# An S4 layer beside a SiLU feed-forward: decays made ahead of the filter's generation, tables in one pass, spectral operands split a step earlier

## The chip, the core and the metric

The kernel runs on one core of one Trainium2 chip. The metric is the device time of one execution in microseconds; of several executions the median counts. A core has five engines that run side by side, each with an instruction queue of its own that is worked in order: TensorE (PE in the profile, its weight loads PEld), VectorE (DVE), ScalarE (ACT), GpSimd (POOL) and SyncE (SP), which here only issues DMAs. They wait for one another through semaphores.

## The reference

```python
xn = _layernorm(x, axis=-1)                       # x: 1 x 2048 x 576
return x + _A_ref(xn, ...) + _B_ref(xn, w1, w2)

# _A_ref: a state-space layer as a long convolution, D = 576 channels, N = 128 states
dt = exp(log_dt)[:, None]; A = A_re + 1j*A_im; Bc, Cc likewise
P = exp((dt*A)[:, :, None] * l)                   # l = 0 .. 2047
K = einsum("dn,dnl,dn->dl", Cc, P, dt*Bc).real    # one filter of 2048 taps per channel
y = irfft(rfft(u, 4096) * rfft(K, 4096))[:2048] + u * Dskip

# _B_ref: feed-forward, F = 4608
out = silu(x @ w1) @ w2
```

All data is float32.

## The kernel before

There are two strands of work. The **feed-forward strand** (`ffn`, L223) is TensorE's main load: nine chunks of 512 hidden columns for each of four row blocks of 512 (two halves of two), 36 blocks of eight steps. `up` makes 512 columns of `ph` with 14 matmuls (L281 to L283), ScalarE applies SiLU (`gf`, L289) and rounds the result to a short float32 form (`gh`, L290), VectorE forms the rest (`gl`, L291). `down` multiplies with w2 (`po`, L306), and VectorE adds each `po` to the accumulator (L310). Every operand is split in a high and a low part (`w1h`/`w1l`, `w2h`/`w2l`), so that each product takes three matmuls. In one block the order is u0, d0, d1, d2, d3, u1, u2, u3, where the u steps belong to the next block.

The **side strand** (`side`, L699) holds all else, in stages:

- `phase0` normalises two row tiles at a time and turns them for the matmuls (`pt`, L118 and L122); tiles 8 to 15 go to DRAM (`dxt`) for the second half.
- `natural` (L370) makes tables from the parameters with states on the free axis: the real rate `lr`, the frequency `f`, the magnitude `rho` and the phase `phi` of C times B. It runs twice, each time over three of the six channel groups (96 x 384 elements an instruction), with a square root and an arctangent on ScalarE, which need other activation tables than SiLU, and turns the tables on TensorE (`ptk`, L452).
- `kgen` (L455) generates the filter in 36 chunks of 16 channels. For a pair of chunks `powers` makes the four decays of each state from `lr`: a product (L484), tanh(x/2) on ScalarE (L485), then (1 + t) / (1 - t) with a reciprocal (L486, L487, L490), then powers up to the seventh (L492 to L494). `head` and the lines after it make sine and cosine tables (L501 to L521), and VectorE multiplies them with the decays into S and C (L522 to L538). TensorE contracts them (`kp`, L558), and turns the result by a small DFT (`z`, L573); the outcome goes to DRAM (`d1k`). Beside it, `spread` does the same first DFT step for the input (`pu`, L149 and L150, to `d1u`).
- `spectral` (L592) has 32 steps. `front(k)` loads and splits the operands from `d1u` and `d1k`, multiplies each with a DFT matrix (`pk`, `pu`), and forms their complex product `y`; the next matmuls (`pb`) turn it back, and it is written to `d2`. `front(k + 1)` stands ahead of the second half of step k.
- `tail` (L637) loads `d2` as `ys` (`conv_load`), and `add_conv` applies the last DFT step (`py`, L691) for the first eight row tiles. For the last eight, `add_conv` is part of the last block's `down`.

What sets the order: `weave` (L31) advances the side strand when the feed-forward strand has made a given share of its 288 steps; the shares of the stages are the tuple `marks` (L701). A planner that runs the program against its own costs then writes the order of each engine's queue; `tc.high_priority()` and `behind(...)` (not before a given instruction) bend it. A pool's tile with `bufs=n` has n buffers, and a writer waits for the readers of the buffer that it takes over.

Of the kernel before, what the change touches and what calls it, by code (L numbers as in the profile page):

```python
# [17 lines left out]
P = 128  # L18
L = 2048
D = 576  # L20
# [21 lines left out]
def kernel(  # L42
# [40 lines left out]
    dr0 = dram.tile([8 * P, D], F32, name="dr0")  # L83

# [6 lines left out]
    nc.vector.memset(halfpi, math.pi / 2)  # L91
    mhalf = cst.tile([P, 2], F32, name="mhalf")
# [76 lines left out]
    def norm(p0, js, xs):  # L169
# [12 lines left out]
        xn = p0.tile([P, 2, D], F32, tag="xn", name="xn")  # L182
# [40 lines left out]
    def ffn():  # L223
# [38 lines left out]
        def split_w2(half, c, t):  # L262
            first = half == 0 and c == 0
            r2 = R2.pop((half, c, t))
            h2 = wp.tile([P, D], F32R, tag="w2h", name="w2h", bufs=FT + 1)
            l2 = wp.tile([P, D], F32R, tag="w2l", name="w2l", bufs=FT + 1)
            with behind(pins["xt_s"] if first else pins["gh"]):
                nc.scalar.copy(h2, r2)  # L268
# [101 lines left out]
    def natural(nat):  # L370
        lrT, fT, rhoT, phiT = (kf[n] for n in ("lr", "f", "rho", "phi"))
        for half in range(2):
            NT = 3
            NP = 96
            ts = slice(half * NT, (half + 1) * NT)

            def load(ap, name):
                t = nat.tile([NP, NT, NS], F32, tag=name, name=name)
                nc.sync.dma_start(t, ap.rearrange("(p t) n -> p t n", t=6)[:, ts, :])
                return t  # L380

            are, aim = load(a_re, "are"), load(a_im, "aim")
            br, bi = load(b_re, "br"), load(b_im, "bi")
            cr, ci = load(c_re, "cr"), load(c_im, "ci")
            dt = nat.tile([NP, NT], F32, tag="dt", name="dt")
            nc.sync.dma_start(dt, log_dt.rearrange("(p t) -> p t", t=6)[:, ts])

            e1 = nat.tile([NP, NT], F32, tag="e1", name="e1")
            e2 = nat.tile([NP, NT], F32, tag="e2", name="e2")
            ec = float(np.float32(math.e))  # L390
            nc.vector.memset(e1, ec)
            nc.vector.tensor_scalar(e2, dt, 1.0 - math.log(ec), 1.0, op0=ALU.mult, op1=ALU.add)
            nc.gpsimd.tensor_tensor(e1, e1, dt, op=ALU.pow)
            nc.vector.tensor_mul(dt, e1, e2)
            dtb = dt.unsqueeze(2).broadcast_to([NP, NT, NS])
            v = nc.vector

            def tl(name):
                return nat.tile([NP, NT, NS], F32, tag=name, name=name)

            dh = nat.tile([NP, NT], F32, tag="dh", name="dh")
            nc.vector.tensor_scalar(dh, dt, 0.5, None, op0=ALU.mult)
            dhb = dh.unsqueeze(2).broadcast_to([NP, NT, NS])
            v.tensor_mul(are, are, dtb)
            nc.scalar.mul(aim, aim, 1.0 / (2 * math.pi))
            v.tensor_mul(aim, aim, dtb)
            pr, pi, t0, t1 = tl("pr"), tl("pi"), tl("t0"), tl("t1")
            v.tensor_mul(pr, cr, br)
            v.tensor_mul(t0, ci, bi)
            v.tensor_sub(pr, pr, t0)  # L410
            v.tensor_mul(pi, cr, bi)
            v.tensor_mul(t0, ci, br)
            v.tensor_add(pi, pi, t0)

            nc.scalar.activation(cr, pr, AF.Abs)
            nc.scalar.activation(ci, pi, AF.Abs)
            v.tensor_tensor(br, cr, ci, op=ALU.max)
            v.tensor_tensor(bi, cr, ci, op=ALU.min)
            v.tensor_scalar(t0, br, 1e-37, None, op0=ALU.max)
            v.reciprocal(t0, t0)  # L420
            v.tensor_mul(t0, t0, bi)
            v.tensor_scalar(t0, t0, 1.0, None, op0=ALU.min)

            v.tensor_mul(t1, t0, t0)
            v.tensor_scalar(t1, t1, 1.0, None, op0=ALU.add)
            nc.scalar.activation(bi, t1, AF.Sqrt)
            rc = tl("rc")
            v.reciprocal(rc, bi)
            v.tensor_mul(rc, rc, t1)
            v.tensor_add(bi, bi, rc)  # L430
            v.tensor_mul(br, br, bi)
            v.tensor_mul(br, br, dhb)

            nc.scalar.activation(t0, t0, AF.Arctan)
            nc.scalar.mul(t0, t0, 1.0 / (2 * math.pi))
            v.tensor_tensor(rc, ci, cr, op=ALU.is_gt)
            v.tensor_scalar(t1, t0, -2.0, 0.25, op0=ALU.mult, op1=ALU.add)
            v.tensor_mul(t1, t1, rc)
            v.tensor_add(t0, t0, t1)
            v.tensor_scalar(rc, pr, 0.0, None, op0=ALU.is_lt)  # L440
            v.tensor_scalar(t1, t0, -2.0, 0.5, op0=ALU.mult, op1=ALU.add)
            v.tensor_mul(t1, t1, rc)
            v.tensor_add(t0, t0, t1)
            v.tensor_scalar(rc, pi, 0.0, None, op0=ALU.is_lt)
            v.tensor_scalar(rc, rc, 2.0, -1.0, op0=ALU.mult, op1=ALU.add)
            v.tensor_mul(t0, t0, rc)
            yield half
            for src, dst in ((are, lrT), (aim, fT), (br, rhoT), (t0, phiT)):
                dv = dst.rearrange("n (p t) -> n t p", t=6)
                pt = pss.tile([P, 512], F32, tag="pss", name="ptk")  # L450
                for i in range(3):
                    nc.tensor.transpose(pt[:, i * NP:(i + 1) * NP], src[:, i, :], ident[:NP, :NP])  # L452
                nc.scalar.copy(dv[:, ts, :], pt[:, :3 * NP].rearrange("n (i p) -> n i p", i=3))

    def kgen():  # L455
        lrT, fT, rhoT, phiT = (kf[n] for n in ("lr", "f", "rho", "phi"))
        with tc.tile_pool(name="kg", bufs=1) as kg:
# [19 lines left out]

            def powers(i):

                ms = kg.tile([P, 2, W, 4], F32, tag="ms", name="ms")  # L480
                md = kg.tile([P, 2, W, 4], F32, tag="md", name="md")
                al = kg.tile([P, 2, W, 4], F32, tag="al", name="al", bufs=2)
                for q in range(2):
                    nc.vector.tensor_mul(split(ms[:, q]), row(vt[:, 65:69], 4), col(lrT, i + q, 4))  # L484
                nc.scalar.activation(ms, ms, AF.Tanh, scale=0.5)  # L485
                nc.vector.tensor_scalar(md, ms, -1.0, 1.0, op0=ALU.mult, op1=ALU.add)  # L486
                nc.vector.reciprocal(md, md)  # L487
                pv = pw.rearrange("n r d k e -> n (r d k) e")
                R = 2 * W * 4
                nc.vector.scalar_tensor_tensor(pv[:, :, 1], ms.rearrange("n r d k -> n (r d k)"), 1.0,  # L490
                                               md.rearrange("n r d k -> n (r d k)"), op0=ALU.add, op1=ALU.mult)
# [100 lines left out]
    def spectral():  # L592
        def front(k):
# [4 lines left out]
            mk = mats[-1][:, k % 2]  # L598
            us, ks = load_split(d1u[k * P:(k + 1) * P, :], "u"), load_split(d1k[k * P:(k + 1) * P, :], "k")
            ka = kl.tile([P, D], F32, tag="ka", name="ka")  # L600
            kb = kl.tile([P, D], F32, tag="kb", name="kb", bufs=1)
# [97 lines left out]
    def side():  # L699
# [10 lines left out]
        with tc.tile_pool(name="kf", bufs=1) as kfp:  # L710
            for n in ("lr", "f", "rho", "phi"):
# [125 lines left out]
```

## Time and profile before

| what | value |
|---|---|
| median of 3 runs | 1140.75 us (1139.23 to 1143.12) |
| profiled execution | 1136.48 us |
| its span, first to last instruction | 1134.7 us, 22990 instructions |
| mean granted TensorE clock | 0.995 |
| DMA | 148.89 MB, mean 131 GB/s |

Busy time of each engine in ten stretches of the profiled execution:

| stretch, us | TensorE | VectorE | ScalarE | what runs beside the feed-forward strand |
|---|---|---|---|---|
| 56 to 85 | 29.00 | 25.45 | 16.46 | tables, row tiles 8 to 15 |
| 85 to 113 | 27.63 | 23.61 | 13.28 | the same |
| 113 to 141 | 26.01 | 23.67 | 17.80 | the same |
| 226 to 255 | 29.00 | 28.81 | 17.58 | filter generation |
| 425 to 453 | 28.00 | 26.59 | 17.12 | the same |
| 652 to 680 | 27.95 | 26.57 | 19.74 | the same |
| 794 to 822 | 28.00 | 22.89 | 22.61 | spectral stage |
| 964 to 992 | 28.00 | 22.21 | 22.61 | the same |
| 1077 to 1106 | 26.41 | 10.43 | 1.20 | tail |
| 1106 to 1134 | 24.65 | 12.36 | 2.36 | last block and stores |

How to read it: a group of the profile is one line, engine and tile; "busy, mean ns | idle before" tells how long the group kept its engine, how long one instruction took, and how long the engine stood still just ahead of it, with what ended that. Matmuls overlap: a matmul of 288 columns is drawn about 297 ns long, but the next one starts sooner, so the distance from one start to the next is what counts. An engine's idle time matters only where it is late for another.

### The profile page before, as it was taken

To read this page: it belongs to the slowest core of one execution; us is meant where nothing else is said; L and a number is where in the kernel's file an instruction comes from. 1 tells how busy PE (TensorE), PEld (TensorE's weight loads), DVE (VectorE), ACT (ScalarE), POOL (GpSimd) and SP (SyncE) were. 2 spreads that over 40 slices of the span, in tenths; PEclk is the share of its full clock that TensorE was granted. 3 is DMA by queue.
4 is the path that set the end of the run, shared out by engine and by line. 5 is a ranking of instruction groups with operands and counts; after the bars stand their busy time and mean duration, and the time that the engine had idled before them with its cause. 6 is when DMAs were issued, how large, how long until landed. Compare 5 with 4: busy or idle time off the path is not lost.

```text
span 1134.7 us, 22990 instructions
## 1 busy us (share of the span) xinstructions
PE 1112.0 (98%) x9184; PEld 1003.2 (88%) x9184; DVE 939.5 (83%) x1649; ACT 708.0 (62%) x1236; POOL 71.7 (6%) x131
## 2 busy tenths in 40 slices
PE   6999999999999999999999999999999999999998
PEld 5988899998989898999898989899999999999957
DVE  7788899999999999999899995587778787777434
ACT  5454646656657666666666674578877777787400
POOL 2100000000000000000000000000000000000021
PEclk9999999999999999999999999999999999999989
DMA  8365312324215143456733242754545454442596
GB/s 261 115 187 187 114 32 79 80 89 99 92 53 127 64 93 96 93 179 173 217 80 109 67 103 57 214 154 141 162 136 152 132 180 144 147 139 74 163 269 196
DMA packets 156203, 148.89 MB, mean 131 GB/s; under 512 B 82512, under 2 KB 123616, under 8 KB 155584
## 3 DMA queue, kind: packets, MB, share of 16 engines
q1 hardware_dynamic: 145872, 110.30, 34.9%
q0 software_dynamic: 9840, 36.24, 9.6%
q8 instruction: 72, 1.18, 0.4%
q10 hardware_dynamic: 384, 0.89, 0.3%
q14 instruction: 35, 0.29, 0.1%
HBM read 102.56 MB, written 44.90 MB: 130 GB/s over the span
## 4 chain that ended last, share of the span: by engine, by line
PE 80%; DVE 7%; DMA 6%; issue 4%; ACT 2%; SPq 1%; ACTq 0%; DVEq 0%; POOLq 0%
PE po L306 34%; PE ph L281 28%; PE kp L558 3%; PE ph L283 2%; PE pk L671 2%; PE ph L282 2%; PE pu L671 2%; PE pb L671 2%; PE z L573 2%; DMA w1r<-in_B_w_dram 1%; PE py L691 1%; DMA ys<-d 1%; PE pu L149 1%; DMA w2r<-in_B_w_dram 1%; DMA acc<-in_A_u_dram 1%
## 5 line engine op out<-in xcount | busy, mean ns | idle before, releaser
L306 PE MATMUL po<-w2h,gh 128*128 128x288 f32 x1152 | 337.4, 297 | 2.5 <-ACT gh L290 2.0
L306 PE MATMUL po<-w2l,gh 128*128 128x288 f32 x1152 | 337.2, 296 | 0.0
L306 PE MATMUL po<-w2h,gl 128*128 128x288 f32 x1152 | 333.5, 296 | 0.6 <-DVE gl L291 0.6
L306 PEld LDWEIGHTS po<-w2h,gh 128*128 128x128 f32 x1152 | 215.2, 188 | 12.2 <-issue 2.8
L306 PEld LDWEIGHTS po<-w2l,gh 128*128 128x128 f32 x1152 | 215.8, 188 | 5.2 <-issue 0.9
L306 PEld LDWEIGHTS po<-w2h,gl 128*128 128x128 f32 x1152 | 214.4, 188 | 1.9 <-DVE gl L291 0.9
L281 PE MATMUL ph<-xh,w1h 128*128 128x512 f32 (+1 forms) x592 | 163.3, 392 | 0.3 <-ACT xh L119 0.3
L281 PE MATMUL ph<-xl,w1h 128*128 128x512 f32 (+1 forms) x592 | 161.6, 388 | 0.0
L281 PE MATMUL ph<-xh,w1l 128*128 128x512 f32 (+1 forms) x592 | 159.9, 386 | 0.0
L310 DVE TENSOR_TENSOR acc<-po,acc 128x288 f32<-128x288 f32 x288 | 126.5, 452 | 28.8 <-PE po L306 27.1
L289 ACT ACTIVATE gf<-ph 128x512 f32<-128x512 f32 (+1 forms) x148 | 86.4, 584 | 97.0 <-PE ph L283 83.9
L281 PEld LDWEIGHTS ph<-xl,w1h 128*128 128x128 f32 x592 | 109.6, 190 | 22.0 <-issue 0.9
L291 DVE TENSOR_TENSOR gl<-gf,gh 128x512 fp32r<-128x512 f32 (+1 forms) x148 | 99.1, 673 | 34.5 <-ACT gh L290 33.9
L281 PEld LDWEIGHTS ph<-xh,w1l 128*128 128x128 f32 x592 | 107.9, 188 | 20.9 <-issue 0.9
L281 PEld LDWEIGHTS ph<-xh,w1h 128*128 128x128 f32 x592 | 106.2, 192 | 16.8 <-issue 0.7
L290 ACT CAST gh<-gf 128x512 fp32r<-128x512 f32 (+1 forms) x148 | 90.0, 609 | 25.7 <-PE po L306 23.1
L517 ACT ACTIVATE c<-th,magic 128x1040 f32<-128x1040 f32 x36 | 42.1, 1169 | 48.2 <-DVE C L538 26.8
L252 DVE TENSOR_TENSOR w1l<-w1r,w1h 128x640 fp32r<-128x640 f32 x72 | 57.0, 818 | 5.7 <-ACT w1h L250 5.5
L519 ACT ACTIVATE c<-th 128x1040 f32<-128x1040 f32 x36 | 38.7, 1076 | 33.3 <-DVE th L518 33.1
L268 ACT CAST w2h<-w2r 128x576 fp32r<-128x576 f32 x72 | 46.9, 674 | 18.0 <-DMA w2r<-in_B_w_dram 14.6
L283 PE MATMUL ph<-x,w1l 128*128 128x512 f32 (+1 forms) x148 | 57.0, 385 | 0.0
L282 PE MATMUL ph<-x,w1h 128*128 128x512 f32 (+1 forms) x148 | 56.9, 385 | 0.0
(176 smaller groups left out, 1869.2 us busy)
## 6 DMA issues: line engine op xcount, KB each, us to landing
w2r<-in_B_w_dram SPq DMA_DIRECT2D x72, 288.0 KB, 3.0
w1r<-in_B_w_dram SPq DMA_DIRECT2D x35, 512.0 KB, 3.9
d1u<-u POOLq DMA_DIRECT2D x32, 288.0 KB, 2.7
d1k<-stage SPq DMA_DIRECT2D x18, 512.0 KB, 8.1
ur<-d1u SPq DMA_DIRECT2D x32, 288.0 KB, 3.6
kr<-d1k SPq DMA_DIRECT2D x32, 288.0 KB, 2.7
d<-yo POOLq DMA_DIRECT2D x32, 288.0 KB, 3.2
ys<-d SPq DMA_DIRECT2D x32, 288.0 KB, 11.0
```

The costliest lines, as they stand in the source:

```text
L252: pins["w1l"] = nc.vector.tensor_sub(l1, src, h1).ins
L268: nc.scalar.copy(h2, r2)
L281: nc.tensor.matmul(ph, w[:, kt, :], v[:, kt, a:e], start=n + kt == 0, stop=False)
L282: nc.tensor.matmul(ph, h1[:, 4, :], x4[:, a:e], start=False, stop=False)
L283: pins["pe"] = nc.tensor.matmul(ph, l1[:, 4, :], x4[:, a:e], start=False, stop=True).ins
L289: nc.scalar.activation(gf, ph, AF.Silu)
L290: pins["gh"] = nc.scalar.copy(gh, gf).ins
L291: pins["gl"] = nc.vector.tensor_sub(gl, gf, gh).ins
L306: pins["pe"] = nc.tensor.matmul(po[:, :HD], G[blk, t][g][:, js], W2[half, c, t][w][:, hs], start=n == 0, stop=n == 3 * FT - 1).ins
L310: nc.vector.tensor_add(acc[j][:, hs], po[:, :HD], acc[j][:, hs])
L517: nc.scalar.activation(c65, th, AF.Identity, bias=magic)
L671: nc.tensor.matmul(dst, st, mv[:, hs], start=n == 0, stop=n == 3 * len(terms) - 1)
```

## The change

The tables are made in one pass over all six groups (96 x 768 elements), and the decays there too: four tanh passes over the turned `lr`, then, in place of the reciprocal of 1 - t, ScalarE's reciprocal square root and its square, with a correction step, three fused VectorE passes for each of four slices. The result goes to DRAM (`dexp`), and `kgen` loads 64 KB of it for each pair of chunks, one pair ahead of use; ScalarE copies it into the buffer for the powers. Sqrt gives way to a reciprocal square root. The passes that need other activation tables stand behind `gh` of a chosen step. Normalised tiles 8 to 15 are written over their own load buffer. In the spectral stage `operands` loads and splits one step further ahead, with three buffers for the splits of `u` and `k` and two for `kb`; the pass that negated half of `kb` is folded into VectorE's product. The marks of the stages are others.

```diff
@@ norm
-        xn = p0.tile([P, 2, D], F32, tag="xn", name="xn")
+        xn = p0.tile([P, 2, D], F32, tag="xn", name="xn") if js[0] < 8 else pairs[js[0]]
@@ natural
-        for half in range(2):
-            NT = 3
...
-            nc.scalar.activation(bi, t1, AF.Sqrt)
-            rc = tl("rc")
-            v.reciprocal(rc, bi)
...
+        NT, NP = 6, 96
...
+        turned(are, lrT)
+        turned(aim, fT)
+
+        ex = nat.tile([P, 4 * D], F32, tag="ex", name="ex")
+        r = nat.tile([P, 4 * D], F32, tag="r", name="r")
+        for k, lag in enumerate((256.0, 64.0, 8.0, 1.0)):
+            nc.scalar.activation(ex.rearrange("n (d k) -> n k d", k=4)[:, k, :], lrT, AF.Tanh, scale=0.5 * lag)
+        yield
+
+        with behind(pins["gh"]):
+            nc.scalar.activation(r, ex, AF.Abs_reciprocal_sqrt, bias=neg1)
+        nc.scalar.activation(r, r, AF.Square)
+        for i in range(0, 4 * D, D):
+
+            c = slice(i, i + D)
+            e = nat.tile([P, D], F32, tag="lrT", name="e")
+            v.scalar_tensor_tensor(e, ex[:, c], 1.0, r[:, c], op0=ALU.subtract, op1=ALU.mult)
+            v.scalar_tensor_tensor(r[:, c], e, 2.0, r[:, c], op0=ALU.add, op1=ALU.mult)
+            v.scalar_tensor_tensor(ex[:, c], ex[:, c], 1.0, r[:, c], op0=ALU.add, op1=ALU.mult)
+        nc.sync.dma_start(dexp, ex)
...
+        with behind(pins["gh"]):
+            last = nc.scalar.activation(t0, t0, AF.Arctan).ins
+        with behind(last):
+            last = nc.scalar.activation(bi, t1, AF.Abs_reciprocal_sqrt).ins
...
@@ kgen
+            def load_bases(i):
+
+                if i < NCK:
+                    bases.append(kg.tile([P, 2, W, 4], F32, tag="eb", name="eb", bufs=2))
+                    nc.sync.dma_start(bases[-1].rearrange("n g c k -> n g (c k)"),
+                                      dexp.rearrange("n (g r) -> n g r", g=2)[:, :, i * CH * 4:(i + 2) * CH * 4])
...
-                for q in range(2):
-                    nc.vector.tensor_mul(split(ms[:, q]), row(vt[:, 65:69], 4), col(lrT, i + q, 4))
-                nc.scalar.activation(ms, ms, AF.Tanh, scale=0.5)
-                nc.vector.tensor_scalar(md, ms, -1.0, 1.0, op0=ALU.mult, op1=ALU.add)
-                nc.vector.reciprocal(md, md)
+                load_bases(i + 2)
+                nc.scalar.copy(pw[:, :, :, :, 1].rearrange("n q (g c) k -> n q g (c k)", g=2),
+                               bases.pop(0).rearrange("n g (q c) k -> n q g (c k)", q=2))
                 pv = pw.rearrange("n r d k e -> n (r d k) e")
                 R = 2 * W * 4
-                nc.vector.scalar_tensor_tensor(pv[:, :, 1], ms.rearrange("n r d k -> n (r d k)"), 1.0,
-                                               md.rearrange("n r d k -> n (r d k)"), op0=ALU.add, op1=ALU.mult)
@@ spectral
+        def front(k):
+            operands(k + 1)
+            mk, us, ks = split.pop(k)
             ka = kl.tile([P, D], F32, tag="ka", name="ka")
-            kb = kl.tile([P, D], F32, tag="kb", name="kb", bufs=1)
+            kb = kl.tile([P, D], F32, tag="kb", name="kb")
...
-                nc.scalar.mul(kb[:64, hs], pk[64:, :HD], -1.0)
...
-                nc.vector.tensor_mul(y2[:64, hs], pu[64:, :HD], kb[:64, hs])
+                nc.vector.scalar_tensor_tensor(y2[:64, hs], pu[64:, :HD], -1.0, kb[64:, hs],
+                                               op0=ALU.mult, op1=ALU.mult)
@@ split_of
+        n = 2 if tag == "y" else 3
@@ side
+    def gate_of(i):
+
+        return (FT + i * 2 * FT + 1) / (2 * NCH * 2 * 2 * FT)
+
-        marks = (0.14, 0.65, 0.875, 0.905, 0.945)
+        marks = (0.13, 0.58, 0.81, 0.915, 0.955)
...
-                for i in range(4):
-                    if i % 2 == 0:
-                        next(nt, None)
-                    yield 0.03 + 0.014 * i
-                    with behind(pins["gl"]):
-                        phase0(pb, (8 + 2 * i, 9 + 2 * i))
-                    yield 0.037 + 0.014 * i
-                next(nt, None)
+                for at, tables in ((0.0, 1), (0.02, 0), (0.035, 0), (gate_of(1), 1), (0.06, 0), (gate_of(2), 1), (0.08, 0), (0.085, 1)):
+                    yield at
+                    if tables:
+                        next(nt, None)
+                    else:
+                        j = next(tiles)
+                        with behind(pins["gl"]):
+                            phase0(pb, (j, j + 1))
```

More of the change, by code (lines that the diff above doesn't have):

```diff
@@ new lines, in natural, with tl, load, turned @@
+        fT, rhoT, phiT = (kf[n] for n in ("f", "rho", "phi"))
+        NT, NP = 6, 96
+        v = nc.vector
+        def tl(name):
+            return nat.tile([NP, NT, NS], F32, tag=name, name=name)
+        def load(ap, name):
+            t = tl(name)
+            nc.sync.dma_start(t, ap.rearrange("(p t) n -> p t n", t=NT))
+            return t
+        def turned(src, dst):
+            dv = dst.rearrange("n (p t) -> n t p", t=NT)
+            for h in range(2):
+                ts = slice(3 * h, 3 * h + 3)
@@ new lines, in natural @@
+        v.tensor_mul(rc, t1, bi)
+        sq = tl("aim")
+        v.tensor_mul(sq, rc, rc)
+        v.tensor_sub(sq, t1, sq)
+        v.tensor_mul(sq, sq, bi)
+        v.scalar_tensor_tensor(bi, rc, 2.0, sq, op0=ALU.mult, op1=ALU.add)
+        v.tensor_mul(br, br, bi)
+        v.tensor_mul(br, br, dhb)
+        with behind(last):
+            nc.scalar.mul(t0, t0, 1.0 / (2 * math.pi))
+        yield
+        v.tensor_tensor(rc, ci, cr, op=ALU.is_gt)
+        v.tensor_scalar(t1, t0, -2.0, 0.25, op0=ALU.mult, op1=ALU.add)
```

148 lines of the change are left out of this document (70 added, 78 removed).

## The prediction

> **What bounds the kernel now.** I read the page's first part, then TensorE's own waits from 100 us on, then busy time by stretch, then the groups of instructions by form, and last the tail in the timeline.
>
> ```profile
> span 1134.7 us, 22990 instructions
> PE 1112.0 (98%) x9184; PEld 1003.2 (88%) x9184; DVE 939.5 (83%) x1649; ACT 708.0 (62%) x1236; POOL 71.7 (6%) x131
> ```
>
> ```profile
> PE py L691 <- DMA ys<-d: 2.4, 2, 1.8
> PE po L306 <- ACT gh L290: 2.0, 1, 2.0
> PE pk L671 <- ACT kh L657: 1.5, 1, 1.5
> PE z L573 <- ACT kt L565: 1.2, 1, 1.2
> ```
>
> TensorE is the bound: after the first 100 us only these four waits of over a microsecond stand between its matmuls, 7.1 us together. The change removes no matmul, so all it can win is such stalls and the slow stretches around them; all it can lose is new ones. Busy time by stretch shows where either can lie (stretch, TensorE, weight loads, VectorE, ScalarE, GpSimd, granted clock, DMA share, GB/s):
>
> ```profile
> 40.00:150.00 110.00, 107.64 (x637) 96.28 (x636) 94.22 (x204) 61.30 (x104) 6.57 (x8) 0.98 0.51 153
> 113.00:125.00 12.00, 10.01 (x48) 8.34 (x47) 10.09 (x16) 8.65 (x15) 0.00 (x0) 0.86 0.22 60
> 171.00:695.00 524.00, 522.59 (x5238) 471.78 (x5237) 495.97 (x778) 340.15 (x509) 21.17 (x39) 1.00 0.38 105
> 730.00:1050.00 320.00, 320.00 (x2020) 297.38 (x2019) 253.80 (x463) 248.32 (x518) 23.93 (x44) 1.00 0.45 141
> ```
>
> From 171 to 695 us (the generation of the filter, kgen) VectorE is busy for 496.0 of 524 us: TensorE is full there, but VectorE has only 28.0 us in hand. From 730 to 1050 us (the spectral stage) TensorE has no gap, and VectorE and ScalarE are idle for 66 and 72 us of 320.
>
> **The tail: 6.4 us won.** Before, the last pb of the spectral stage and the first py are close together in TensorE's order, and the loads of ys begin only when d2 is written. The page's DMA issues, the chain of waits (start, length) and the timeline (start, length, engine, line):
>
> ```profile
> ys<-d SPq DMA_DIRECT2D x32, 288.0 KB, 11.0
> ```
>
> ```profile
> 127.34 2.73 PE ph L281 x12
> 132.67 3.88 PE po L306 x29
> ```
>
> ```profile
> 1105.43 0.29 PE L306 MATMUL po<-w2h,gl 128*128 128x288 f32 x1
> 1105.65 0.71 PE L691 MATMUL py<-ys,s 64*32 64x288 f32 x16
> ...
> 1106.54 0.29 PE L306 MATMUL po<-w2l,gh 128*128 128x288 f32 x1
> ```
>
> The two lines from the chain of waits give the undisturbed pace: 3.88 / 29 = 0.134 us for a po matmul, 2.73 / 12 = 0.2275 for a ph matmul. In the timeline, an undisturbed group of 16 py records sits between two po matmuls (the one at 1106.30 lies between the rows): 1106.54 - 1105.43 - 2 x 0.134 = 0.84 us. Now the stretch from the first py wait to the last matmul, for po, ph and py alone:
>
> ```profile
> 1077.40:1130.40 53.00, 25.68 (x169) 23.25 (x167) 6.76 (x15) 0.94 0.91 246
> 1077.40:1130.40 53.00, 12.60 (x42) 8.40 (x42) 1.80 (x3) 0.94 0.91 246
> 1077.40:1130.40 53.00, 14.30 (x256) 3.98 (x256) 13.40 (x32) 0.94 0.91 246
> ```
>
> 169 x 0.134 + 42 x 0.2275 + 16 x 0.84 = 22.6 + 9.6 + 13.4 = 45.6 us of work took 53.0: 7.4 us are lost, the 2.4 us of waits, and 0.06 x 53 = 3.2 us of clock among them. In the new order, 45 us of TensorE's matmuls (counted at the paces above) stand between the last pb and the first py, where 17 us stood; 45 us is four times the 11.0 us that a ys load takes, and the first py groups have po and ph matmuls between them. So the loss should go, but for about 1 us (a group whose PSUM tile VectorE hasn't read yet): I count 6.4 of the 7.4. What hides the loads is that gap; should kgen run late, the gap stays, since TensorE's order is fixed.
>
> **The tables: 2 us won.** Before, the two halves of the tables drop Arctan and Sqrt, with three table loads, anywhere into ScalarE's queue; gf and gh queue behind them, and TensorE stands for 2.0 us for gh. Behind that the clock of the 113 to 125 row is 0.86: 0.14 x 12 = 1.7 us more, 3.7 in all. The new order has 6 table loads for 7, and pins (`gate_of`, `behind(pins["gh"])`) put each block of them behind u0's gh, ahead of the four down steps d0 to d3, which need no new gh.
>
> ```profile
> L250 ACT CAST w1h<-w1r 128x640 fp32r<-128x640 f32 x72 | 48.8, 726 | 11.5 <-DMA w1r<-in_B_w_dram 11.5
> ...
> L519 ACT ACTIVATE c<-th 128x1040 f32<-128x1040 f32 x36 | 38.7, 1076 | 33.3 <-DVE th L518 33.1
> ...
> L426 ACT ACT_TABLE_LOAD x2 | 2.6, 1283 | 0.0
> ```
>
> The longest block holds two table loads, two passes over 128x2304 (at most 2304/1040 x 1.076 = 2.38 each) and, in the new order, three weight splits between them (0.73 each): 2.57 + 4.77 + 2.18 = 9.5 us. Its cover is d0 to d3, 96 x 0.134 = 12.9 us. Where the cover is gone, its whole 9.5 us shows at gh. The Trainium skill (ScalarE: Activation LUTs, "What ACT_TABLE_LOAD costs") adds about 1.38 us of drain to each switch of 1283 ns; by that the block is 12.3 us, the cover is used up, and this term would be 0 instead of 2. The rows show the 1283 ns alone.
>
> VectorE is the doubt of this stage. It is busy for 94.2 of 110 us between 40 and 150 us. The decays add 12 passes over 128x576, the one pass without Sqrt drops two reciprocals:
>
> ```profile
> L617 DVE TENSOR_TENSOR y<-y,y 128x576 f32<-128x576 f32 x32 | 24.1, 752 | 0.1
> ...
> L428 DVE RECIPROCAL rc<-bi 96x384 f32<-96x384 f32 x2 | 5.1, 2550 | 5.3 <-ACT bi L426 5.3
> ```
>
> 12 x 0.752 - 5.1 = 3.9 us more (the fused form is priced as the plain one, see below), and kgen starts 6 us earlier in TensorE's order: 9.9 us against 15.8 idle. It fits, but adds to PSUM and weight splits will sometimes be 1 or 2 us late. Of the 3.7 us I therefore take 2.0. The loads for the tables are twice as long in one go, and stand on SyncE's queue ahead of the next w1 loads, whose users come over 10 us later; log_dt now comes first; storing xn from its own load buffer holds the next load of x back by one tile. I cost these at nothing; if w1 came late, up would wait.
>
> **kgen: 2.3 us lost.** Each pair of chunks loses the step that made its decays, and gains one ScalarE copy of about the tanh's size and one load of 64 KB.
>
> ```profile
> L487 DVE RECIPROCAL md<-md 128x128 f32<-128x128 f32 x18 | 17.0, 946 | 0.0
> ...
> L490 DVE SCALAR_TENSOR_TENSOR pw<-ms,md 128x128 f32<-128x128 f32 x18 | 7.3, 405 | 0.0
> ...
> L484 DVE TENSOR_TENSOR ms<-vt,lrT 128x64 f32<-128x64 f32 x36 | 6.4, 220 | 0.0
> ...
> L486 DVE TENSOR_SCALAR md<-ms 128x128 f32<-128x128 f32 x18 | 3.9, 219 | 0.1
> ```
>
> That is 34.6 us of VectorE for 18 steps, 30.8 for the 16 inside the stretch. But the marks also squeeze the stage: between the first and the last kp TensorE's new order has 218 fewer po and 114 fewer ph matmuls, 218 x 0.134 + 114 x 0.2275 = 55 us less cover, so 469 us. VectorE leaves less of its own work behind with them:
>
> ```profile
> L310 DVE TENSOR_TENSOR acc<-po,acc 128x288 f32<-128x288 f32 x288 | 126.5, 452 | 28.8 <-PE po L306 27.1
> ...
> L291 DVE TENSOR_TENSOR gl<-gf,gh 128x512 fp32r<-128x512 f32 x140 | 95.7, 687 | 32.3 <-ACT gh L290 31.7
> ```
>
> 218/12 x 0.439 + 114/14 x 0.684 = 13.6 us (the shared weight splits are left out, on the cautious side). So 496.0 - 30.8 - 13.6 = 451.6 us of VectorE work in 469: 17 us in hand for 28.0 before, 1.0 us for each of the 17 pairs instead of 1.6. What used the 28.0 us were not waits for TensorE's po:
>
> ```profile
> DVE S L537 <- ACT th L520: 8.6, 10, 1.5
> DVE w1l L252 <- ACT w1h L250: 5.5, 3, 3.0
> DVE gl L291 <- ACT gh L290: 4.8, 5, 1.2
> DVE C L522 <- PE kp L558: 2.6, 5, 1.2
> ```
>
> Of these, S behind the sine is fixed (VectorE makes th, ScalarE takes abs and sine, VectorE goes on); in the new order the work between is shorter for half of the chunks, and I put this wait at 14 us for 8.6. The other three, 12.9 us, shrink when VectorE itself is later. Bounds: 0 lost if they shrink wholly and the sine waits stay as they were (451.6 + 8.6 is under 469); 10.6 lost if all 28.0 stay. Between them, 14 fixed and half of the other three stay: 451.6 + 14 + 6.5 = 472.1, 3.1 over 469. I round this to 3.5 lost, and the 1.2 us wait of z for kt goes, since the new order sets z 1.5 us further behind kp: net 2.3.
>
> The weighing of a clock rule belongs here. The 113 to 125 row shows a stall of 2.0 us answered by 1.7 us of lost clock. The Trainium skill (TensorE: Matmul & The Clock Gate, "What's actually happening") sets half rate after an idle window of about 3.4 us; by that, stalls of 1 to 3 us in kgen would cost themselves alone, and the sum stands; by the row, one of 2 us or more costs 1.7 more, which the upper end holds.
>
> **The spectral stage: nothing.** Splitting a step ahead, kb with two buffers and one ScalarE pass less take from engines that wait:
>
> ```profile
> L501 DVE TENSOR_TENSOR th<-vt,fT 128x1040 f32<-128x1040 f32 x36 | 44.5, 1236 | 0.1
> L518 DVE SCALAR_TENSOR_TENSOR th<-c,th 128x1040 f32<-128x1040 f32 x36 | 44.4, 1233 | 1.6 <-ACT c L517 1.2
> ...
> L610 ACT ACTIVATE kb<-pk 64x288 f32<-64x288 f32 x64 | 26.2, 409 | 1.7 <-DVE y L616 0.6
> ```
>
> The 26.2 us of L610 fall off ScalarE, idle for 72 us there; the sign moves into a fused form, which costs what the plain one does (1233 and 1236 ns). TensorE has no gap to close. The 1.5 us wait of pk for kh ends a chain from the last stage over the stores of d1k, the add of dskip and the first kr load; the change leaves it, and TensorE's order has as many matmuls in it as before.
>
> **The sum.** Against the profiled execution (span 1134.7 us, 1136.48 in all): -6.4 - 2.0 + 2.3 = -6.1, so 1130.4. The three runs have a median of 1140.75, 4.3 above it; the same step from there gives 1134.6, which I forecast. A difference under 0.3%, about 3.4 us, can hardly be told from none.
>
> **The rivals.**
> *VectorE keeps all its waits in kgen.* All 28.0 us stay, 10.6 us late instead of 3.5: 1134.6 + 7.1 = 1141.7, no change. For: every wait before is on ScalarE, and ScalarE serves the same chain. Against: it was idle for 184 of 524 us. Chance 0.19.
> *The hand-over of the decays makes kgen VectorE's own (slower).* `pw` has one buffer. VectorE reads it, ScalarE's copy may write only then, VectorE's next square waits for the copy. On ScalarE gf, gh and the sine of the other chunk are queued behind the waiting copy, and VectorE's gl behind those. In the new order 1.8 to 7.6 us of VectorE's work cover the hand-over; where 2.5 us or less do (7 of 17), a copy behind the four passes of a chunk (four of about 1.1 us, as L519) comes 2 us or more late. It decides once waits pass 1.0 us a pair. At the old 1.6, 0.3 for the shorter sine cover and 0.5 for this, 2.4 a pair, 24 us are lost: 1134.6 + 20 = 1155. Chance 0.17.
> *Nothing is lost in kgen.* Waits shrink into the 17 us: 1134.6 - 3.5 = 1131. Chance 0.12.
> *The tables stall more than before.* VectorE late for adds, 4 us instead of a gain of 2: 1140.6, no change. Chance 0.06.
> That the change does not do what it says is ruled out for the order, which shows the removed and moved instructions.
>
> My forecast has 0.46. Faster by over 0.3%: it and the third, and a little off for its spread toward 1137.3: 0.46 + 0.12 = 0.58. The same: 0.19 + 0.06 = 0.25. Slower: 0.17. The forecast's own range is 1130 to 1138; to hold 8 in 10 it must reach down to 1129 (the tail's 7.4 and the stage's 3.7 whole, nothing lost in kgen: 1140.75 - 7.4 - 3.7 - 1.2 = 1128.5) and up to 1147, half way into the slower rival.
>
> **What would show it.** Right: no wait of py for ys; no half clock near 1080 us; no wait of over 1 us for gh before 150 us; kgen's stretch from first to last kp 469 to 474 us with VectorE at 96%; TensorE without gaps in the spectral stage. Wrong: kp waiting for the tables C and S by over 5 us in all, VectorE waiting on pw for the copy, or adds of po that hold TensorE's PSUM tiles in the table stage.

## The result, and the profile after

The changed kernel is slower: 1144.83 us median (1140.48 to 1147.33, 12 runs) against 1139.66 (1138.76 to 1143.12, 12 runs) of the kernel before, a ratio of 1.0043 with a 95% interval of 1.0031 to 1.0055. Its profiled execution took 1142.79 us, so 6.3 us of span are to be found. All ratios below are taken against runs of the kernel before on the same chip, since its own median moved between 1137.3 and 1139.7 us from chip to chip.

The page's first part of the changed kernel, and TensorE's waits from 100 us on (total, times, longest):

```profile
span 1141.0 us, 22849 instructions
PE 1113.4 (98%) x9184; PEld 1002.1 (88%) x9184; DVE 918.2 (80%) x1540; ACT 685.0 (60%) x1171; POOL 74.8 (7%) x130
```

```profile
PE po L309 <- ACT gh L293: 2.9, 1, 2.9
PE ph L284 <- ACT gf L292: 2.5, 1, 2.5
PE z L613 <- ACT kt L605: 1.7, 1, 1.7
PE pu L720 <- ACT kb L657: 1.6, 1, 1.6
```

Work did leave the engines: VectorE is busy for 21 us less, ScalarE for 23 us less. The wait of py for ys is gone. Two waits for ScalarE's gf and gh are new. Busy time by stretch shows when (columns as before):

```profile
40.00:150.00 110.00, 107.67 (x648) 96.34 (x647) 97.20 (x180) 66.99 (x101) 9.56 (x7) 1.00 0.48 146
168.00:640.20 472.20, 469.95 (x5033) 423.24 (x5032) 453.75 (x665) 323.67 (x488) 21.21 (x39) 1.00 0.42 112
695.00:982.50 287.50, 287.50 (x1829) 267.90 (x1828) 230.64 (x420) 200.83 (x412) 23.37 (x43) 1.00 0.49 145
998.00:1012.00 14.00, 14.00 (x91) 13.08 (x90) 5.63 (x10) 4.25 (x7) 0.00 (x0) 1.00 0.90 258
1012.00:1024.00 12.00, 12.00 (x69) 10.69 (x68) 2.73 (x5) 1.90 (x3) 0.00 (x0) 1.00 1.08 221
1024.00:1040.00 16.00, 10.63 (x49) 8.66 (x48) 4.60 (x8) 4.59 (x8) 0.00 (x0) 0.89 0.73 169
1053.00:1128.00 75.00, 75.00 (x571) 59.12 (x573) 30.14 (x63) 15.84 (x26) 9.75 (x20) 1.00 0.45 120
```

From 1024 to 1040 us TensorE stands for 5.4 of 16 us and its clock is 0.89; the loss follows a stretch in which the DMA engines are full (0.90, then 1.08). What they are full of is seen in SyncE's queue: the timeline of DMA issues of the changed kernel (start, length of issuing, count).

```profile
998.97 2.17 SPq L689 DMA_DIRECT2D r<-dr  x4
1001.17 12.67 SPq L727 DMA_DIRECT2D ys<-d  x12
1014.63 0.35 SPq L262 DMA_DIRECT2D w2r<-in_B_w_dram  x1
...
1019.92 5.80 SPq L727 DMA_DIRECT2D ys<-d  x4
1025.83 11.25 SPq L262 DMA_DIRECT2D w2r<-in_B_w_dram  x3
```

As soon as the last row of d2 is written, four r0 loads (576 KB each) and sixteen ys loads (288 KB each), 6.9 MB, are issued, and weight loads come between and behind them. The chain of waits (start, length) has the consequence:

```profile
1003.82 10.74 DMA ys<-d
1014.63 11.09 DMA w2r<-in_B_w_dram
1025.83 9.41 DMA w2r<-in_B_w_dram
```

A w2r load lands in 3.3 us as the median of its 72 in the page's DMA issues; these two took 11.09 and 9.41. ScalarE's split of it into w2h waits for the load, the activations gf and gh wait behind that in ScalarE's queue, and TensorE waits for those. ScalarE's timeline shows the first case (in brackets, how long it stood idle and what ended that):

```profile
1025.75 0.67 ACT L271 CAST w2h<-w2r 128x576 fp32r<-128x576 f32 x1 [7.79 <-DMA w2r<-in_B_w_dram]
1026.33 0.59 ACT L292 ACTIVATE gf<-ph 128x512 f32<-128x512 f32 x1
```

TensorE's next ph matmul starts at 1026.97 us, when this gf is done. In the kernel before, the same burst came just behind the last weight load, which landed in 2.7 us, so that none was held up:

```profile
1061.76 0.33 SPq L259 DMA_DIRECT2D w2r<-in_B_w_dram  x1
1065.69 1.93 SPq L641 DMA_DIRECT2D r<-dr  x4
```

### The profile page after: what moved, and what is told of

It is laid out like the page before. It is cut to its first block, busy times and chain, and to the rows that moved or that the text cites. A ratio compares the mean times of both kernels' runs of the same rounds, so it can differ in the third digit from the quotient of the medians.

```text
span 1141.0 us, 22849 instructions
## 1 busy us (share of the span) xinstructions
PE 1113.4 (98%) x9184; PEld 1002.1 (88%) x9184; DVE 918.2 (80%) x1540; ACT 685.0 (60%) x1171; POOL 74.8 (7%) x130
## 4 chain that ended last, share of the span: by engine, by line
PE 49%; issue 20%; DVE 16%; DMA 10%; ACT 3%; POOL 1%; SPq 1%; DVEq 0%; POOLq 0%; ACTq 0%
PE po L309 21%; PE ph L284 16%; DMA w2r<-in_B_w_dram 3%; PE pb L720 2%; PE pk L720 2%; PE pu L720 2%; DMA dxt<-xt 2%; DVE acc L313 2%; DVE gl L294 1%; PE ph L285 1%; PE ph L286 1%; DVE w2l L273 1%; DVE th L558 1%; PE py L740 1%; DVE C L577 1%
## 5 line engine op out<-in xcount | busy, mean ns | idle before, releaser
L273 DVE TENSOR_TENSOR w2l<-w2r,w2h 128x576 fp32r<-128x576 f32 x72 | 53.6, 751 | 17.8 <-ACT w2h L271 17.7
L255 DVE TENSOR_TENSOR w1l<-w1r,w1h 128x640 fp32r<-128x640 f32 x72 | 56.6, 820 | 2.3 <-ACT w1h L253 2.2
```

Source lines behind the costliest of these rows:

```text
L255: pins["w1l"] = nc.vector.tensor_sub(l1, src, h1).ins
```

## Experiments

The experiments weigh four theories. Theory Q: the burst stands ahead of the weight loads on the one queue. Its rivals: B, the burst's bytes fill the DMA engines, whichever queue issues them; K, the kernel is slow because the new marks squeeze kgen; S, the tables and the spectral edits cost the time. The first four runs share a chip.

**Another queue for the tail's loads.**

```diff
-            nc.sync.dma_start(r0, dr0[...])
+            nc.gpsimd.dma_start(r0, dr0[...])
...
-                nc.sync.dma_start(yss[j][64 * h:64 * h + 64],
+                nc.gpsimd.dma_start(yss[j][64 * h:64 * h + 64],
```

> The changed kernel, with the tail's loads (four of r0, all of ys) issued by GpSimd's DMA queue and not by SyncE's. Theory Q (the burst of tail loads stands ahead of the weight loads on SyncE's one queue): the four waits for w2r go, the offset of TensorE between 1009 and 1049 us falls from 8.0 us to 2 or less, and the time is 6 to 8 us under the changed kernel's, 1137 to 1139. Theory B (the burst fills the DMA engines, whichever queue issues it): the weight loads are late all the same, and at most 2 us come back: 1143 to 1145. Theory K (what the squeezed kgen costs makes the kernel slow, the tail costs what it always did): no change, 1144.8.

Measured: 1146.85 us, ratio 1.0068 (1.0056 to 1.0080). Q falls. The time lies above the ranges of B and K too, but the weight loads are late all the same, as B has it. The wait between loads and splits, TensorE's wait, and the one w2r issued between 1006 and 1007.1 us (KB, time to landing):

```profile
ACT w2h L271 <- DMA w2r<-in_B_w_dram: 15.5, 2, 13.6
PE ph L284 <- ACT gf L292: 8.9, 1, 8.9
w2r<-in_B_w_dram SPq DMA_DIRECT2D x1, 288.0 KB, 21.6
```

On SyncE's own queue, now clear of the tail, w2r was issued 8 us earlier than in the changed kernel (1006.6 us) and took 21.6 us: it landed later, not earlier. The Trainium skill (DMA: Bandwidth & Descriptors, "Issuing engines are not separate DMA queues") says that DMAs of SyncE and GpSimd run on the same 16 DMA engines and interleave; this run agrees, with 21.6 us for a load on a queue clear of the burst.

**Loads spread in the program.** `AHEAD` from 6 to 2, r0 loaded one step ahead, buffers as they were (eight of ys, four of r0).

```diff
-    AHEAD = 6
+    AHEAD = 2
...
-            yss[j] = yp.tile([P, 4, HD], F32, tag="ys", name="ys", bufs=AHEAD + 2)
+            yss[j] = yp.tile([P, 4, HD], F32, tag="ys", name="ys", bufs=8)
```

> The changed kernel, with the tail's loads spread: one of r0 and two pairs of ys in the first burst (5 transfers in place of 16), the others one step at a time as the adds go on; same queue, same buffers. Theories Q and B agree here: the weight loads meet a third of the burst, 4 to 8 us come back, 1137 to 1141, unless py now waits for its ys (each up to the 6.7 us of one load, less the distance of two steps). Theory K: no change, 1144.8.

Measured: 1147.01 us, ratio 1.0063 (1.0047 to 1.0080), a miss for all the theories. DMA issues of this run between 1000 and 1040 us:

```profile
ys<-d SPq DMA_DIRECT2D x15, 288.0 KB, 11.0
w2r<-in_B_w_dram SPq DMA_DIRECT2D x3, 288.0 KB, 10.6
```

The edit hardly spread the burst: fifteen ys loads are still issued in these 40 us. Where a load stands in the program did not hold it back as long as a buffer was free, so this run says nothing against B.

**Old marks.**

```diff
-        marks = (0.13, 0.58, 0.81, 0.915, 0.955)
+        marks = (0.14, 0.65, 0.875, 0.905, 0.945)
```

> The changed kernel with the marks of the kernel before (0.14, 0.65, 0.875, 0.905, 0.945). Theories Q and B: the burst falls behind the last weight loads as in the kernel before, so the tail's 3.3 us go, py waits for ys again; kgen has its old stretch of 524 us and 31 us less of VectorE's work, so it loses 2 to 4 us less than before's 6.1: 1136 to 1138.5. Theory K: the marks are all of the loss, kgen's 2.0 go, and the tail has no part: 1138 to 1140, with the tail's loss in the trace at what it is in the changed kernel. Theory S (the tables and the spectral edits cost the time, not the marks): 1143 to 1146.

Measured: 1147.20 us, ratio 1.0065 (1.0052 to 1.0077). All theories missed; S, the nearest, by over 1 us. SyncE's queue in the timeline, and TensorE's largest wait:

```profile
1055.26 2.20 SPq L689 DMA_DIRECT2D r<-dr  x4
1057.50 18.89 SPq L727 DMA_DIRECT2D ys<-d  x16
1077.17 0.35 SPq L262 DMA_DIRECT2D w2r<-in_B_w_dram  x1
```

```profile
PE po L309 <- ACT w2h L271: 8.3, 1, 8.3
```

The burst comes some 10 us earlier than in the kernel before, at 1055 and not 1066 us, and so ahead of the last w2r and not behind it. K falls: with the old marks the same stall is there, in another place.

**New marks for the kernel before.**

```diff
-        marks = (0.14, 0.65, 0.875, 0.905, 0.945)
+        marks = (0.13, 0.58, 0.81, 0.915, 0.955)
```

> The kernel before with the marks of the changed one, and nothing else. The filter's generation has 496.0 - 13.6 = 482 us of VectorE's work in 469 us, so it is late by 13 us if every wait goes and by 41 if the 28 us stay: 1153 to 1181 by theories Q and B, in which the decays made ahead paid for the new marks. Theory K, with marks as the whole of the loss: 1144 to 1147. The tail's burst stands ahead of the weight loads here too.

Measured: 1157.24 us, ratio 1.0150 (1.0131 to 1.0169). The stretch from the first to the last kp:

```profile
174.60:669.00 494.40, 481.47 (x5068) 431.24 (x5068) 475.61 (x742) 323.05 (x484) 21.11 (x39) 0.99 0.40 106
```

It takes 494.4 us where the changed kernel needs 472.2. Of these 22 us some 7 are work: the stretch holds 15 po and 21 ph matmuls more than the changed kernel's, 15 x 0.134 + 21 x 0.2275 = 6.8 us at the prediction's paces. So the decays made ahead are worth about 15 us at these marks. At the old marks, the generation takes no less time with them than without: 531.8 us in the run before this one, 525.1 in the kernel before, and the 31 po and 10 ph matmuls more of the former are 6.4 us. That the burst would hold up weight loads here too did not come true: TensorE waits for no weight in this run's tail.

What was left was B, and against it theory O: w2h is late for a reason of ScalarE's order, not of the loads. The next four runs share a chip. All have two buffers of ys and two of r0, so that a load can only be issued when an add has freed one.

**Few tail buffers.**

```diff
-            r0 = yp.tile([P, 2, D], F32, tag="r0", name="r0", bufs=4)
+                r0s[j] = yp.tile([P, 2, D], F32, tag="r0", name="r0", bufs=2)
...
-    AHEAD = 6
+    AHEAD = 1
...
-            yss[j] = yp.tile([P, 4, HD], F32, tag="ys", name="ys", bufs=AHEAD + 2)
+            yss[j] = yp.tile([P, 4, HD], F32, tag="ys", name="ys", bufs=2)
```

> The changed kernel with fewer buffers for the tail: two of ys (for 8) and two of r0 (for 4), so that only two r0 loads and four ys loads can be under way before the first add; same queue, same marks, TensorE's order as in the changed kernel but for a few neighbours. Theory B (each weight load stands in the DMA engines behind the bytes that the tail has queued, whatever the queue): 2.4 MB in place of 7 MB stand ahead, about 13 us at the 190 KB per us of the runs so far, over by 1012 us, before w2r is due; the waits of 5 to 12 us for w2r go. TensorE's offset from the last pk to the first py falls from 8.1 us to 1 or less: 1137 to 1138.5 against the changed kernel's 1144.8. Theory O (ScalarE's order and the split of w2r into w2h are late for another reason, loads or not): 1144 to 1147. Against both: py may wait for ys with so few ahead, up to 4 us in all.

Measured: 1136.75 us, ratio 0.9992 (0.9979 to 1.0005), 0.51% below the changed kernel's ratio. The same stretches as above, and the loads issued from 1005 to 1007.2 us:

```profile
1012.00:1024.00 12.00, 12.00 (x69) 10.69 (x68) 4.76 (x8) 4.26 (x7) 0.00 (x0) 1.00 0.24 69
1024.00:1040.00 16.00, 16.00 (x112) 14.18 (x111) 4.06 (x9) 3.04 (x5) 0.00 (x0) 1.00 0.04 14
```

```profile
w2r<-in_B_w_dram SPq DMA_DIRECT2D x1, 288.0 KB, 6.3
```

The DMA engines are at 0.24 where they were at 1.08, TensorE has no gap and the whole clock. TensorE's order is the same but for a few neighbours, so times compare directly: the last pk begins at 982.5 us in both, the first py at 1047.2 before and 1039.1 now. 8.1 us are back in these two executions; by the ratios, which rest on two chips, it is 0.51% or 5.8 us. O falls, and with it S as the cause of these 8 us: no table and no spectral edit was touched.

**Few buffers, GpSimd's queue** (the two edits together).

> The kernel with few tail buffers, its r0 and ys loads issued on GpSimd's queue. Theory B with the queue irrelevant: as the one on SyncE's queue, within 1 us. If loads that wait for a buffer hold weight loads behind them on SyncE's queue, this one is faster than that by the waits for w1r and w2r that it shows, 1 to 5 us. Theory O: 1144 to 1147.

Measured: 1135.80 us, ratio 0.9984 (0.9972 to 0.9996): not to be told from the run before it. The queue does not matter in either direction.

**Few buffers, slower generation** (`marks = (0.13, 0.58, 0.81, 0.915, 0.955)` to `(0.13, 0.62, 0.84, 0.915, 0.955)`; the text's 0.14 is a slip for 0.13).

> The kernel with few tail buffers, with marks 0.14, 0.62, 0.84 for 0.13, 0.58, 0.81: the filter's generation has some 46 us more of cover. If the 2 us that the changed kernel loses there come from the squeeze, and the step at the end of the spectral stage stays away, this is 2 us under the kernel with few tail buffers: 1135 to 1136.5. If the loss there is fixed, no difference. Theory O: 1142 to 1146.

Measured: 1135.15 us, ratio 0.9972 (0.9960 to 0.9985). 2.3 us under the run with few buffers by the ratios, the size that was expected; the intervals overlap by a little, so this is likely and not certain. The trace does not put it in the generation: the stretch from the first to the last kp is 505.8 us for 472.3, 33.5 more, and holds 126 po and 76 ph matmuls more, 34.2 us. Only 0.7 us of loss went there, and where the rest came from is not shown.

**Few buffers, old marks.**

> The changed kernel with few tail buffers and the marks of the kernel before. In the run with the old marks and all buffers TensorE was 0.9 us ahead of the kernel before until the last pk, and lost 20 us from there, with one wait of 8.3 us for w2r. Theory B: that wait goes, and the clock loss behind it; 1136 to 1139. Theory O: it stays, 1146 to 1148. The spectral stage ends 57 us later than with the new marks, so the 16 pairs of ys, four of r0 and the stores of out share the last 85 us: py may wait for ys.

Measured: 1135.54 us, ratio 0.9982 (0.9972 to 0.9992), where the old marks with all buffers gave 1.0065. B holds a second time: with the burst limited, the wait for w2r is gone there too.

The next four, on another chip, ask what the parts are worth by themselves.

**The kernel before with few buffers alone** (the same edit).

> The kernel before with the few tail buffers alone (two of ys, two of r0, loads one step ahead); marks, tables, decays and spectral stage as they were. There the burst falls behind the last weight load, so by theory B no wait for w2r can go: same as before within 0.2%, 1136 to 1140, py waiting for ys as before or 1 to 2 us more. If few buffers are worth 5 us in any version (a rival to B, theory F: shorter bursts help py itself), 1133 to 1135.

Measured: 1148.24 us, ratio 1.0078 (1.0065 to 1.0091), a miss. TensorE's wait, and the stretch from the first py to the end:

```profile
PE py L696 <- DMA ys<-d: 10.6, 6, 3.4
```

```profile
1073.00:1138.70 65.70, 55.10 (x488) 38.85 (x487) 22.70 (x52) 4.78 (x8) 10.71 (x22) 0.90 0.79 218
```

In this order the adds of py follow each other closely, and the loads of two buffers can't keep up: 10.6 us of waits and 0.10 x 65.7 = 6.6 us of clock. Few buffers are no gain in themselves; they need a longer tail, which the new marks give, or the new spectral stage with the old marks (the run before this one).

**Old spectral stage, few buffers, new marks** (`front` and `split_of` as in the kernel before).

> The changed kernel with few tail buffers, and the spectral stage of the kernel before (operands split one step ahead only, one buffer of kb, the extra ScalarE pass). If the spectral edits are worth nothing, as forecast: the same as the run with few tail buffers, ratio 0.999, and 3 to 5 us from the last kp to the last pk. If splitting a step ahead is what makes the start of the stage late (pu waits 0.5 to 1.6 us for kb there): 2 us faster. If it hides ScalarE's work: slower by 2 us or more, with waits of pb or pu in the stage.

Measured: 1135.04 us, ratio 0.9965 (0.9952 to 0.9977), 0.27% below its partner with the new stage, as the second case has it. But that one ran on the chip before, so the 3 us are not certain.

**Old spectral stage, few buffers, old marks.**

> The tables in one pass and the decays made ahead, alone: the kernel with few tail buffers and the old marks, and the spectral stage of the kernel before. Against the kernel before with few buffers it shows what tables and decays are worth at the old marks. If VectorE's 31 us fewer in the generation pay only where the stage is squeezed: no difference from it beyond 1.5 us, 1136 to 1139. If they pay at any marks: 2 to 4 us faster than it.

Measured: 1154.23 us, ratio 1.0131 (1.0116 to 1.0146), against 0.9982 with the new stage, a miss by 15 us. The last pk begins at 1050.9 us here and at 1039.9 with the new stage: the edits end the stage 11 us earlier in TensorE's order. Here the tail is tight without them and py waits for ys, 13.0 us in all. This run can't say what tables and decays are worth alone.

**Both corrections.** Marks (0.14, 0.62, 0.83, 0.92, 0.953), three buffers of ys and two of r0, loads on GpSimd's queue, new spectral stage.

> The changed kernel with marks 0.14, 0.62, 0.83, 0.92, 0.953, three buffers of ys and two of r0, the tail's loads on GpSimd's queue. Loss by stage from the runs so far, if each keeps its least: tables as they are, generation as with the slower marks, no late start of the spectral stage, no wait of w2r, and py a little later than there so that its waits for ys (2.5 us) go: 2 to 3 us under the run with slower generation, ratio to before 0.995, 1132 to 1134.

Measured: 1134.87 us, ratio 0.9962 (0.9948 to 0.9976): faster than both kernels, but above the expected range, and not to be told from the slower generation (0.9972) or the old spectral stage (0.9965) with few buffers alone.

Two more runs, on a fourth chip, for what was open.

**Four buffers of ys** (`AHEAD` 3, two of r0).

> The kernel with few tail buffers, but with four buffers of ys for two: two r0 loads and eight of ys in the first burst, 3.5 MB in place of 2.4 and 7. Theory B: at 190 KB per us the burst is over near 1017 us; the first w2r, which took 6.3 us with 2.4 MB ahead and 11.1 to 21.7 with all, takes 10 to 12, and its split ends a few us before TensorE needs it: 0 to 2 us lost between the last pk and the first py, 1136 to 1139. If the delay goes with the count of buffers for another reason (theory O), half of the 8 us: 1140 to 1141.

Measured: 1135.01 us, ratio 0.9983 (0.9971 to 0.9995). The w2r issued between 1006 and 1007 us:

```profile
w2r<-in_B_w_dram SPq DMA_DIRECT2D x1, 288.0 KB, 9.7
```

It is late by 6 us, and TensorE loses nothing: 56.7 us from the last pk (980.2 us) to the first py (1036.9), 56.6 with two buffers. So O's half of the 8 us is not there. 3.5 MB are still under cover; 6.9 MB are not. Where between them the loss begins was not tried.

**The best marks with the old spectral stage.**

> The kernel with the best marks so far, few tail buffers and loads on GpSimd's queue, with the spectral stage of the kernel before. If the spectral edits cost 2 to 3 us, as the pair with the new marks has it: ratio to before 0.994, 1131 to 1133. If that was chance: the same ratio as its partner, 0.996, 1134 to 1135. If they help here: over 1136.

Measured: 1141.03 us, ratio 1.0043 (1.0025 to 1.0061), against 0.9962 with the new stage. So the new stage is worth 9 us with these marks, 17 us with the old ones, and nothing or a loss of 3 us with the changed kernel's marks, where the tail is long anyway; each of the three compares ratios from two chips. The profile shows where this execution lost time (stretches from the start of the tail; py waits once for 0.6 us and once for 1.8 up to 1060 us):

```profile
1040.00:1056.00 16.00, 15.37 (x93) 11.86 (x92) 4.91 (x9) 5.72 (x10) 6.40 (x10) 1.00 0.84 218
1056.00:1080.00 24.00, 22.16 (x126) 14.67 (x125) 7.45 (x15) 2.33 (x4) 10.38 (x18) 0.64 0.94 239
1080.00:1141.00 61.00, 61.00 (x473) 47.07 (x472) 24.52 (x51) 10.35 (x17) 17.00 (x30) 1.00 0.52 142
```

2.5 us of waits came with (1 - 0.64) x 24 = 8.6 us of lost clock. But this execution took 1147.80 us, 6.8 above the median of its twelve, and its mean clock is 0.991 where nine of them have 0.995 or more. So the lost clock explains why this one was slow; what makes the median slower than with the new stage is not shown.

## Why the prediction was wrong

The measured 1144.83 us lie inside the prediction's wide range of 1129 to 1147, but that is luck: its upper end was set for the hand-over of pw, of which the trace shows no wait. All its signs of being right came true but for a wait of 1.6 us (pu for kb) at the start of the spectral stage, and the kernel was slower. None of the signs looked at the 45 us between the last pb and the first py.

**The tail: this is the step that failed.** Forecast 6.4 us won. The first half held: py no longer waits for ys, and counted at the prediction's own paces the part from the first py to the end loses 2.5 us and not 7.4. The rows of the changed kernel for po, ph and py:

```profile
1047.10:1136.40 89.30, 45.07 (x313) 41.96 (x312) 11.79 (x26) 1.00 0.44 117
1047.10:1136.40 89.30, 33.90 (x138) 25.20 (x138) 5.97 (x10) 1.00 0.44 117
1047.10:1136.40 89.30, 14.10 (x256) 3.41 (x256) 13.52 (x32) 1.00 0.44 117
```

313 x 0.134 + 138 x 0.2275 + 13.4 = 86.8 of 89.3 us; 4.9 us won. (The 2.5 us left are likely the count's own: with few tail buffers the same stretch, 1039.1 to 1128.6 us, has no gap and the whole clock, and the count leaves 2.5 us there too. So the 7.4 us may have been sized too high as well; its waits and clock alone are 5.6.) What the step left out is what the earlier loads collide with. It called the 45 us between the last pb and the first py cover for the ys loads, and did not ask who else needs the DMA engines in those 45 us. The change moved the burst from behind the last weight load to the middle of a block's weights, and that cost 8.0 us: 8.1 us come back when only the buffers are fewer. Net 3.1 us lost for 6.4 won. None of the rivals named it. Yet with the collision gone the ratio is 0.9992, and the forecast of 6.1 us won asks for 0.9946: the other steps below were off as well.

**The tables.** Forecast 2.0 us won, measured 0. The first kp comes 6.2 us earlier (174.2 and 168.0 us), which is the 6 us by which it stands earlier in TensorE's order, and no more. In the other profiles it lies at 173.0 and 174.6 us with the old tables, and from 166.9 to 170.0 with the new ones, so 2 us either way could hide here, but no clear gain. The wait for gh of 2.0 us is gone and the clock is 1.00, but po now waits up to 1.5 us for w2h. ScalarE in the timeline of the changed kernel:

```profile
94.42 1.28 ACT L460 ACT_TABLE_LOAD   x1
95.72 0.85 ACT L460 ACTIVATE t<-t 96x768 f32<-96x768 f32 x1
96.58 1.28 ACT L462 ACT_TABLE_LOAD   x1
97.88 0.84 ACT L462 ACTIVATE bi<-t 96x768 f32<-96x768 f32 x1
98.63 0.66 ACT L271 CAST w2h<-w2r 128x576 fp32r<-128x576 f32 x1
```

The prediction put d0 to d3 ahead of the tables' blocks as cover since they need no new gh. They also need w2h, and this split stands behind the block of 4.3 us. Each table load takes 1.28 us and the activation starts 0.01 to 0.02 us behind it, so the weighing with the drain of the Trainium skill (ScalarE: Activation LUTs, "What ACT_TABLE_LOAD costs") went the way of the row.

**The generation.** Forecast 2.3 us lost, a stretch of 472.1 us with 451.6 us of VectorE's work; measured 472.2 and 453.75. Against the kernel before, 472.2 is 525.1 less the 55.1 us of moved cover, and 2.2 us over. That the numbers meet is in part luck: the wait of z for kt did not go (1.7 us), and the waits for the sine are 8.2 us where the forecast had 14. VectorE's hand-over of pw did not show. The mechanism stands in the main: VectorE's relief was spent on the marks (about 15 us by the fourth run). That the 2.2 us are the price of the squeeze is not shown, since the seventh run's trace gives back only 0.7 of them.

**The spectral stage.** Forecast nothing. From 695 us to its end TensorE has no gap, as said. But the edits end the stage 6.5 to 11 us earlier (last pk at 982.5 for 989.0 us with the new marks, 1039.9 for 1050.9 with the old), and this sets how much room the tail has: with few buffers and the old marks, 168 po and 89 ph matmuls stand between the first and the last py, 147 and 42 without the edits. By the ratios this is worth 17 us there, and 9 with the marks of the last two runs. The prediction used the new order's distance without asking which edit made it.

**The sum.** 3.1 for the tail, 0 for the tables and 2.2 for the generation are 5.3 of the 6.3 us; the last 1.0 seem to lie in TensorE's first waits of the spectral stage (pu for kb, 1.6 us, where pk waited 1.5 for kh) and in a first matmul that starts a little later. That split of 1.0 is argued from two profiles and not shown.

## What to carry to other kernels

Before a gap in one engine's order is called cover for a transfer, list what else uses the DMA engines in that gap: loads are issued as soon as their buffers are free, and all the buffers of a prefetch fire at once, ahead of the small loads that the bound engine needs next. The number of buffers is the tool that limited such a burst here, not the queue and not the place in the program; but it must leave enough ahead for the consumer's own pace, since the same two buffers cost 0.8% in the tight order. A relief on one engine is worth nothing until the schedule spends it, and what it is spent on should be priced as a change of its own.

## What the runs showed of the hardware

A 288 KB load landed in 3.3 us as a rule, in 6.3 with 2.3 MB of other loads just ahead, 9.7 with 3.5 MB, 11.1 in the middle of 6.9 MB on its own queue, and 21.6 when the 6.9 MB came from another queue. The last is more than an even interleaving would give: SyncE's queue held 0.9 MB of weights at that time, and twice that at the burst's own pace (6.9 MB and some 1.5 MB of weights in 38 us, about 0.22 MB per us) is an estimate of 8 to 9 us. Why the queue with the burst got more is seen in the packets of that run from 1012 to 1028 us (packets, MB; q0 is GpSimd's queue, q1 SyncE's):

```profile
q0 software_dynamic: 757, 2.78, 77.3%
q1 hardware_dynamic: 757, 0.91, 27.2%
```

The two queues moved equally many packets, not equally many bytes, and a packet of the burst is three times as large (3.7 KB for 1.2). So a weight load on a queue of its own got a quarter of the bytes, and 0.9 MB took some 16 us.

The clock answered short waits unevenly. In the changed kernel a wait of 2.5 us was followed by four microseconds at 0.57; the wait of 2.9 us right behind by none (1.00); in the last run waits of 0.6 and 1.8 us went with 24 us at 0.64. The records of the granted clock show only 1.0 and 0.5, and from 20 us to the last matmul each stretch at 0.5 lasts a multiple of 3.41 us: once 3.41 us in the changed kernel (from 1028.3 us), five times that in the last run (1059.8 to 1076.8), up to six times in the run with the old spectral stage and the old marks. What decides how many is open. The Trainium skill (TensorE: Matmul & The Clock Gate, "What's actually happening") gives about 3.4 us of idleness as the condition; these waits were shorter.

```profile
1028.00:1032.00 4.00, 4.00 (x12) 3.14 (x11) 0.29 (x1) 0.07 (x1) 0.00 (x0) 0.57 1.09 223
1036.00:1040.00 4.00, 3.50 (x19) 3.02 (x20) 3.11 (x6) 1.56 (x3) 0.00 (x0) 1.00 0.28 74
```
